# Scores of a head pair as 64-row matmuls on K without zero padding, in a windowed attention kernel with a maxout FFN behind it

## The chip, the core and the metric

The kernel runs on one NeuronCore of a Trainium2 chip. The metric is the time of one execution in device microseconds, as the median over several runs. TensorE appears in the profile as two rows: PE for its matmuls and PEld for the loads of the stationary operand (the weights). The other engines are VectorE (DVE), ScalarE (ACT), GpSimd (POOL) and SyncE (SP), which issues most of the DMAs.

## The reference

Attention over 4 batches, 8 heads, 768 positions and 64 elements per head. A query sees the first 4 positions (the sinks) and the last 128. The heads of a position are then joined to a row of 512 and go through an FFN that takes the elementwise maximum of three products.

```python
scores = scale * np.matmul(q, k.transpose(0, 1, 3, 2))
keep = is_sink | ((rel >= 0) & (rel < 128))      # rel = query position - key position
a = softmax(np.where(keep, scores, -1e9))
x = np.matmul(a, v)          # heads joined: (3072, 512)
h = np.maximum(np.maximum(x @ w1, x @ w2), x @ w3)   # w1, w2, w3: (512, 768)
out = h @ w_out                                      # (768, 512)
```

## The kernel before

The 3072 rows are cut into 12 chunks of 256 positions, three chunks to a batch. Chunk c = 0 of a batch (chunks 0, 3, 6 and 9) has no keys before it. Each chunk goes through the same steps, each a function that emits its instructions when it is called; the order in which the steps are called is written out by hand in strings of short names, and each engine works through its instructions in that order. In "Sb0 Fa1" the first letter is the step, the second says which of the chunks in flight, and the rest is the step's number.

- **K, Q** (`prep`, chunks 0 to 3): K and Q of one half of the heads are transposed on TensorE into PSUM. ACT copies Q to `qT`; `place_k` copies K to `kz` on DVE. For the later chunks **D** (`turn`) transposes by DMA and **E** calls `place_k` on the result.
- **S** (`score`): the scores of one head, with keys on the partitions and queries on the free axis. Q of a pair of heads lies in `qT` with one head on partitions 0 to 63 and the other on 64 to 127. K lies in `kz` twice as wide: for each of the two heads a block of all 128 partitions, where that head's 64 carry K and the other 64 carry zeros. So a matmul with all 128 rows gives the scores of one head. A step has a matmul of 128 columns against the keys of the chunk before (L246, not where c = 0), one of 256 (L248) and one of 128 (L249), into a PSUM tile `st`. ACT takes the exponential of the tile into `e_sb` (L255), and after the second head of a pair DVE multiplies the pair by the mask (L258).
- **Z** (`sink_score`): the scores of the four sinks for all heads (L264) from `ks`, which `sink_k` fills from K at a batch's first chunk.
- **A** (`av`): scores times V into `o_ps` for four heads and 128 positions (L278 for the sinks, L286 for the rest), then a reciprocal and a multiply on DVE (L291, L294) into `x_sb`.
- **T** (`xpose`): `x_sb` transposed on TensorE (L306) and copied by ACT (L307).
- **F** (`ffn_h`): nine steps to a chunk, each eight matmuls of 256 columns (L319). ACT copies the product of w1 to `h_sb` (L323); those of w2 and w3 are joined by DVE with a maximum (L325).
- **Y** (`ffn_y`): the last product (L330), copied by ACT (L335) and stored.

From chunk 2 on one iteration of the loop runs F and Y of a chunk, S, Z, A and T of the next, and the placing of K of the one after. S steps stand singly between F steps:

```python
run("Sb0 Sb1 Fa0 Sb2 Fa1 Sb3 Fa2 Zb Sb4 Fa3 Sb5 Ab00 Fa4 Sb6 Ab01 Fa5 Sb7 Fa6 Fa7 Ab10 "
    "Fa8 Ab11 Ec Ya0 Tb0 Tb1 Ya1", a=i, b=i + 1, c=i + 2)
```

PSUM is given out in three pools that hand their buffers round: `ps_s` with two buffers (scores and sink scores), `ps_o` with two (A, T and the transposes) and `ps_f` with four (F, Y and, in the first two chunks, one score tile of a pair). `e_sb` has six buffers.

Before the loop the strings are longer, the casts of the inputs to bf16 run on POOL and DVE (L181, L189), and the weights arrive. `warm` puts in matmuls whose result nobody reads. The zeros of `kz` are written once: two blocks by DVE (L99), four by ACT (`zeros_act`, L117) and six by POOL (L99).

Of the kernel before, what the change touches and what calls it, by code (L numbers as in the profile page):

```python
# [9 lines left out]
F32 = mybir.dt.float32  # L10
BF16 = mybir.dt.bfloat16
AF = mybir.ActivationFunctionType
ALU = mybir.AluOpType
# [3 lines left out]
def kernel(  # L17
# [13 lines left out]
    nc = tc.nc  # L31
# [8 lines left out]
    scale = 1.0 / (D ** 0.5)  # L40
    NP = H // 2
    CPB = S // 256
# [8 lines left out]
    with tc.manual_schedule():  # L51
        const = tc.alloc_tile_pool(name="const", bufs=1)
        raw = tc.alloc_tile_pool(name="raw", bufs=3)
        work = tc.alloc_tile_pool(name="work", bufs=2)
        ps_s = tc.alloc_tile_pool(name="ps_s", bufs=2, space=bass.MemoryType.PSUM)
        ps_o = tc.alloc_tile_pool(name="ps_o", bufs=2, space=bass.MemoryType.PSUM)
        ps_f = tc.alloc_tile_pool(name="ps_f", bufs=4, space=bass.MemoryType.PSUM)
# [3 lines left out]
        def load(ci, gate=None):  # L61

            b, c = divmod(ci, CPB)
            t0 = c * 256
            eng = nc.sync
            qk = raw.tile([128, 2, 2, 512], F32, tag="qk_raw", name="qk_raw")
            vr = raw.tile([128, 2, H, D], F32, tag="v_raw", name="v_raw")
            if gate is not None:
                gate.memset(qk[0:1, 0, 0, 0:1], 0.0)
            for g in range(2):  # L70
                for j, src in ((0, k), (1, q)):
                    eng.dma_start(  # L72
                        out=qk[:, j, g].rearrange("p (h i d) -> p h (i d)", h=4, d=D),
                        in_=src[b, 4 * g:4 * g + 4, t0:t0 + 256]
                            .rearrange("h (p i) d -> p h (i d)", i=2))
            eng.dma_start(
                out=vr.rearrange("p n h d -> p (n h d)").rearrange("p (h x) -> p h x", h=H),
                in_=v[b, :, t0:t0 + 256].rearrange("h (p i) d -> p h (i d)", i=2))
            raws[ci] = (qk, vr)
# [8 lines left out]
        load(1)  # L88


        kz = [const.tile([128, 2, NP, 256], BF16, name=f"kz{i}") for i in range(2 * CPB)]
        qT = [const.tile([128, 2, NP, 128], BF16, name=f"qT{i}") for i in range(2 * CPB)]
        ve = [const.tile([128, S // 128, H, D + 1], BF16, name=f"ve{i}") for i in range(2)]
        ks = [const.tile([128, NP * 130], BF16, name=f"ks{i}") for i in range(2)]
        vs = const.tile([128, B, H, D + 1], BF16, name="vs")

        def zeros(i, c, eng):
            for h in range(2):
                eng.memset(kz[CPB * i + c][64 - 64 * h:128 - 64 * h, h], 0.0)  # L99

        ident = const.tile([128, 128], BF16, name="ident")
        make_identity(nc, ident)
# [1 line left out]
        def warm(n):  # L104

            wp = ps_f.tile([128, 128], F32, tag="f", name="warm")
            for _ in range(n):
                nc.tensor.matmul(wp, lhsT=ident, rhs=ident, start=True, stop=True)  # L108

        zc = const.tile([128, 1], BF16, name="zc")  # L110
        nc.vector.memset(zc, 0.0)
        zeros(0, 0, nc.vector)

        def zeros_act(i):
            for h in range(2):
                hp = slice(64 - 64 * h, 128 - 64 * h)
                nc.scalar.copy(kz[i][hp, h], zc[hp].unsqueeze(1).to_broadcast([64, NP, 256]))  # L117

        zeros_act(1)
        nc.scalar.copy(vs.rearrange("p b h d -> p (b h d)"), zc.to_broadcast([128, B * H * (D + 1)]))  # L120
        nc.vector.memset(ve[0][:, :, :, D:D + 1], 1.0)
        nc.vector.memset(ks[0], 0.0)
# [2 lines left out]
        msk = const.tile([128, 4, 128], BF16, name="msk")  # L125
        nc.gpsimd.memset(msk[:, 0:2], 1.0)
        for i in range(2):
            for slot, op, sign in ((1, ALU.is_ge, 1), (0, ALU.is_gt, -1)):
                m = msk[64 * i:64 * i + 64, slot].rearrange("p (i t) -> p i t", i=2)
                nc.gpsimd.affine_select(  # L130
                    out=m, in_=m, compare_op=op, fill=0.0, base=-sign * i,
                    pattern=[[sign, 2], [2 * sign, 64]], channel_multiplier=-2 * sign)
        nc.gpsimd.tensor_copy(msk[:, 2:4], msk[:, 0:2])
        msk0 = const.tile([128, 3, 128], BF16, name="msk0")
# [61 lines left out]

        def place_k(ci, src, pairs):

            for h in range(2):
                hp = slice(64 * h, 64 * h + 64)  # L200
                nc.vector.tensor_copy(  # L201
                    kz[ci % (2 * CPB)][hp, h, pairs].rearrange("p a (n i t) -> p i (a n) t", n=2, i=2),
                    src[hp].rearrange("p i a (n t) -> p i (a n) t", n=2))

        def prep(ci, j, g):

# [21 lines left out]
        def sink_k(b):  # L228
            kv = ks[b % 2].rearrange("p (a y) -> p a y", y=130)[:, :, 0:8 * n_sink]
            for h in range(2):  # L230
                for i in range(2):
                    nc.vector.tensor_copy(
                        kv.rearrange("p a (t i x) -> p i a t x", i=2, x=8)[:, i, :, :, h],
                        kz[b * CPB % (2 * CPB)][:, h, :, 64 * i:64 * i + n_sink // 2])

        es = {}

        def score(ci, hd):
            b, c = divmod(ci, CPB)
            p, h = divmod(hd, 2)  # L240
            kh = kz[ci % (2 * CPB)][:, h, p]
            qh = qT[ci % (2 * CPB)][:, :, p].rearrange("p i (n t) -> p n i t", n=2)
            st = (ps_f.tile([128, 4, 128], F32, tag="f", name="st") if ci < 2 and h == 1 else
                  ps_s.tile([128, 4, 128], F32, tag="s", name="st"))
            if c > 0:
                nc.tensor.matmul(st[:, 0], lhsT=kz[(ci - 1) % (2 * CPB)][:, h, p, 128:256],  # L246
                                 rhs=qh[:, 0], start=True, stop=True)
            nc.tensor.matmul(st[:, 1:3], lhsT=kh[:, 0:128], rhs=qh, start=True, stop=True)  # L248
            nc.tensor.matmul(st[:, 3], lhsT=kh[:, 128:256], rhs=qh[:, 1],  # L249
                             start=True, stop=True)  # L250
            if h == 0:
                es[ci, p] = work.tile([128, 2, 4, 128], BF16, tag="e", bufs=6, name="e_sb")
            e = es[ci, p]
            lo = 0 if c > 0 else 1
            nc.scalar.activation(e[:, h, lo:], st[:, lo:], AF.Exp, scale=scale)  # L255
            if h == 1:
                m = (msk if c > 0 else msk0).unsqueeze(1).to_broadcast([128, 2, 4 - lo, 128])
                nc.vector.tensor_tensor(out=e[:, :, lo:], in0=e[:, :, lo:], in1=m, op=ALU.mult)  # L258

        def sink_score(ci):  # L260
            b, c = divmod(ci, CPB)
# [82 lines left out]
        def step(op):  # L344

            name, ci, arg = op[0], int(op[1:3]), op[3:]
            if ci >= NCH:
                return
            if name in "KQ":
                prep(ci, int(name == "Q"), int(arg))  # L350
            elif name == "D":
                turn(ci)
            elif name == "E":
                place_k(ci, kTs.pop(ci), slice(0, NP))
            elif name == "S":
                score(ci, int(arg))
            elif name == "Z":
                if ci % CPB:
                    sink_score(ci)
                elif ci > 0:  # L360
                    sink_k(ci // CPB)
            elif name == "A":
                av(ci, int(arg[0]), int(arg[1]))
            elif name == "T":
                xpose(ci, int(arg))
            elif name == "F":
                ffn_h(ci, int(arg))
            elif name == "Y":
                ffn_y(ci, int(arg))

        def run(text, **at):
            for tok in text.split():
                c = at[tok[1]]
                step(f"{tok[0]}{c:02d}{tok[2:]}")
# [21 lines left out]
        load_w(1)  # L396
        load_w(2)
        load(2, nc.gpsimd)
        run("Sa0 Sa1 Ka1", a=0)
        warm(3)  # L400
        run("Qa1", a=0)
        warm(4)
        run("Sa2 Sa3 Sa4 Sa5", a=0)
        warm(3)
        run("Aa00", a=0)
        warm(2)
        run("Sa6 Sa7 Aa01", a=0)
        warm(2)
        run("Kb0 Qb0 Aa10", a=0, b=1)
        warm(2)  # L410
        run("Aa11", a=0)
        sink_k(0)
        run("Sb0 Sb1 Ta0 Sb2", a=0, b=1)
        warm(6)
        run("Kb1 Qb1", b=1)
        cast_v(1, 1, nc.vector)
        run("Sb3 Ta1 Zb Sb4 Sb5 Sb6 Sb7", a=0, b=1)
        warm(6)
        run("Ab00 Ab01", b=1)
        zeros_act(2)  # L420
        warm(4)
        run("Fa0 Ab10 Fa3 Ab11 Fa6 Tb0 Tb1", a=0, b=1)
        cast_qk(2, 0, 0, nc.gpsimd)
# [4 lines left out]
        cast_v(2, 0, nc.gpsimd)  # L428
        cast_v(2, 1, nc.gpsimd)
        load(3, nc.gpsimd)  # L430
        run("Fa1 Fb0 Fb3 Fb6 Fa4 Fa7 Fb1 Fb4 Fb7 Kc0 Qc0 Fa2 Kc1 Qc1 Fa5 Sc0 Sc1 Fa8 Zc Sc2 Fb2",
            a=0, b=1, c=2)
        for c in range(CPB):
            zeros(1, c, nc.gpsimd)
        nc.gpsimd.memset(ks[1], 0.0)
        nc.gpsimd.memset(ve[1][:, :, :, D:D + 1], 1.0)
        cast(3)
        for b in range(1, B):
            sink_v(b)
        run("Sc3 Sc4 Fb5 Ac00 Sc5 Fb8 Ac01 Sc6 Ya0 Sc7 Ya1", a=0, b=1, c=2)  # L440
        load(4)
        cast(4)
        run("Ac10 Ac11 Yb0 Tc0 Kd0 Tc1 Qd0 Yb1 Kd1 Qd1", b=1, c=2, d=3)
# [1 line left out]
        for i in range(2, NCH):  # L445
            run("Dc", c=i + 2)
            if i + 3 < NCH:
                load(i + 3)
                cast(i + 3)
            run("Sb0 Sb1 Fa0 Sb2 Fa1 Sb3 Fa2 Zb Sb4 Fa3 Sb5 Ab00 Fa4 Sb6 Ab01 Fa5 Sb7 Fa6 Fa7 Ab10 "  # L450
                "Fa8 Ab11 Ec Ya0 Tb0 Tb1 Ya1", a=i, b=i + 1, c=i + 2)

        for pool in (ps_f, ps_o, ps_s, work, raw, const):
            pool.release()
# [35 lines left out]
```

## Time and profile before

| | before |
|---|---|
| median of 4 runs | 197.01 us (196.56 to 197.84) |
| the profiled execution | 197.5 us, of which the span from first to last instruction is 195.8 us |
| granted TensorE clock, mean | 0.985 |
| PE / PEld busy | 183.4 us (94%) / 150.5 us (77%) |
| DVE / ACT / POOL busy | 127.3 us (65%) / 108.6 us (55%) / 79.3 us (41%) |
| DMA moved | 32.85 MB, 168 GB/s in the mean |

Times in the profile's rows are those of single instructions from start to end. On TensorE the ends are modelled, and a matmul's time holds the way through the array, so that matmuls that follow each other overlap in the rows; the distance from one start to the next is what a matmul costs in a full stream. The rows of ACT and DVE overlap a little in the same way. The profiled execution took 197.5 us against the median of 197.01.

### The profile page before, as it was taken

The numbers are of one execution on the slowest core, as the hardware profiler recorded it, in microseconds if no ns is written. First come the engines' busy times: TensorE is split into PE (matmuls) and PEld (weight loads), VectorE is DVE, ScalarE is ACT, GpSimd is POOL, SyncE is SP. The second block draws the span as 40 slices with busy tenths as digits, with TensorE's granted clock in tenths as the row PEclk, the third lists the DMA queues.
The fourth block names the chain that finished last, engine by engine and source line by source line (L and its number), as shares of the span: only waits on it lengthen the run. The fifth ranks groups of instructions, "written<-read, shape, count | busy, mean of one in ns | idle before, by whom it ended". The sixth has DMA issues, their size and how long they took to land.

```text
span 195.8 us, 4740 instructions
## 1 busy us (share of the span) xinstructions
PE 183.4 (94%) x1904; PEld 150.5 (77%) x1916; DVE 127.3 (65%) x275; ACT 108.6 (55%) x202; POOL 79.3 (41%) x133
## 2 busy tenths in 40 slices
PE   7778999999899999999999999999999999999990
PEld 7657788884697798798797897897886996996850
DVE  4699825885379379469479469468476585583520
ACT  8748951453762862862753863863754745744221
POOL 7399105999965543602702625504505500000000
PEclk9978999999999999999999999999999999999997
DMA  5969999893999699298499899497497740400404
GB/s 160 306 186 145 160 216 287 122 279 108 260 280 240 192 200 281 57 170 238 138 111 279 211 153 291 107 224 222 96 224 220 147 71 0 107 3 0 110 2 107
DMA packets 60774, 32.85 MB, mean 168 GB/s; under 512 B 18512, under 2 KB 57680, under 8 KB 60752
## 3 DMA queue, kind: packets, MB, share of 16 engines
q1 hardware_dynamic: 58368, 29.40, 63.2%
q0 software_dynamic: 2384, 3.15, 10.2%
q8 instruction: 15, 0.25, 0.5%
q14 instruction: 7, 0.06, 0.1%
HBM read 25.20 MB, written 6.29 MB: 161 GB/s over the span
## 4 chain that ended last, share of the span: by engine, by line
PE 69%; DMA 9%; POOL 6%; DVE 6%; ACT 2%; issue 2%; SPq 2%; POOLq 0%; DVEq 0%
PE h_ps L319 37%; PE y_ps L330 15%; DMA qk_raw<-in_q_dram 6%; PE o_ps L286 5%; PE st L248 4%; DMA v_raw<-in_v_dram 3%; DVE h_sb L325 3%; DVE e_sb L258 2%; POOL ve L189 2%; PE xt_ps L306 2%; PE st L249 2%; SPq L72 2%; PE sk L264 2%; PE st L246 2%; POOL qk_bf L181 1%
## 5 line engine op out<-in xcount | busy, mean ns | idle before, releaser
L319 PE MATMUL h_ps<-xT,w 128*128 128x256 bf16 x864 | 108.0, 273 | 0.2 <-DMA w<-in_moe_w_dram 0.2
L319 PEld LDWEIGHTS <-w 128*128 128x128 bf16 x864 | 80.2, 98 | 9.3 <-issue 0.4
L255 ACT ACTIVATE e_sb<-st 128x512 bf16<-128x512 f32 (+1 forms) x96 | 52.6, 575 | 19.2 <-PE st L249 18.7
L325 DVE TENSOR_TENSOR h_sb<-h_sb,h_ps 128x512 bf16<-128x512 bf16 x72 | 49.2, 683 | 15.8 <-PE h_ps L319 14.0
L258 DVE TENSOR_TENSOR e_sb<-e_sb,msk 128x1024 bf16<-128x1024 bf16 (+1 forms) x48 | 35.0, 734 | 35.6 <-ACT e_sb L255 35.0
L181 POOL CAST qk_bf<-qk_raw 128x512 bf16<-128x512 f32 x44 | 27.9, 646 | 60.4 <-DMA qk_raw<-in_k_dram 42.8
L189 POOL CAST ve<-v_raw 64x512 bf16<-64x512 f32 x46 | 31.7, 688 | 12.9 <-DMA v_raw<-in_v_dram 9.8
L330 PE MATMUL y_ps<-wo,h_sb 128*128 128x512 bf16 x132 | 34.2, 379 | 0.9 <-DVE h_sb L325 0.3
L335 ACT COPY y_sb<-y_ps 128x512 f32<-128x512 f32 x24 | 14.1, 587 | 37.4 <-PE y_ps L330 31.1
L323 ACT CAST h_sb<-h_ps 128x512 bf16<-128x512 f32 x36 | 21.3, 592 | 12.3 <-PE h_ps L319 12.3
L248 PE MATMUL st<-qT,kz 128*128 128x256 bf16 x96 | 25.3, 275 | 0.8 <-ACT qT L214 0.5
L286 PE MATMUL o_ps<-ve,e_sb 128*128 128x65 bf16 x352 | 20.6, 196 | 2.2 <-DVE e_sb L258 1.1
L330 PEld LDWEIGHTS <-h_sb 128*128 128x128 bf16 x144 | 12.8, 98 | 12.1 <-DVE h_sb L325 1.3
L294 DVE TENSOR_TENSOR x_sb<-o_ps,rc 128x256 bf16<-128x256 f32 x48 | 20.4, 425 | 1.7
L286 PEld LDWEIGHTS <-e_sb 128*128 128x128 bf16 x352 | 17.7, 99 | 4.3 <-DVE e_sb L258 2.0
L249 PE MATMUL st<-qT,kz 128*128 128x128 bf16 x96 | 20.8, 220 | 0.0
L246 PE MATMUL st<-qT,kz 128*128 128x128 bf16 x64 | 14.2, 221 | 0.4 <-ACT e_sink L269 0.3
L307 ACT COPY xT<-xt_ps 128x512 bf16<-128x512 bf16 x24 | 13.3, 601 | 0.5 <-PE xt_ps L306 0.5
L248 PEld LDWEIGHTS <-kz 128*128 128x128 bf16 x96 | 9.4, 98 | 3.5 <-DVE kz L201 0.8
L249 PEld LDWEIGHTS <-kz 128*128 128x128 bf16 x96 | 9.5, 99 | 1.1 <-issue 0.5
L201 DVE COPY kz<-kT 64x1024 bf16<-64x1024 bf16 x16 | 9.6, 599 | 0.3
L108 PE MATMUL warm<-ident 128*128 128x128 bf16 x76 | 8.3, 268 | 1.4 <-POOL ident masks.py:199 1.4
(45 smaller groups left out, 116.0 us busy)
## 6 DMA issues: line engine op xcount, KB each, us to landing
qk_raw<-in_k_dram SPq DMA_DIRECT2D x24, 256.0 KB, 4.2
qk_raw<-in_q_dram SPq DMA_DIRECT2D x24, 256.0 KB, 4.4
v_raw<-in_v_dram SPq DMA_DIRECT2D x12, 512.0 KB, 5.8
out_dram<-y_sb SPq DMA_DIRECT2D x22, 256.0 KB, 3.4
w<-in_moe_w_dram POOLq DMA_DIRECT2D x3, 768.0 KB, 7.7
wo<-in_moe_w_out_dram POOLq DMA_DIRECT2D x2, 384.0 KB, 6.4
out_dram<-y_sb SPq DMA_DIRECT2D x4, 128.0 KB, 2.3
kT<-qk_bf SPq DMA_TRANSPOSE x8, 5.9
```

The source lines that it names most:

```text
L181: eng.tensor_copy(dst.rearrange("p i (h d) -> p h i d", d=D), src)
L189: eng.tensor_copy(dst[64 * i:64 * i + 64], src[64 * n:64 * n + 64, :, i])
L248: nc.tensor.matmul(st[:, 1:3], lhsT=kh[:, 0:128], rhs=qh, start=True, stop=True)
L249: nc.tensor.matmul(st[:, 3], lhsT=kh[:, 128:256], rhs=qh[:, 1], start=True, stop=True)
L255: nc.scalar.activation(e[:, h, lo:], st[:, lo:], AF.Exp, scale=scale)
L258: nc.vector.tensor_tensor(out=e[:, :, lo:], in0=e[:, :, lo:], in1=m, op=ALU.mult)
L286: nc.tensor.matmul(o[:, hh], lhsT=es[ci, p][:, h, sl], rhs=ve[b % 2][:, n, 2 * p + h], start=(c == 0 and x == 0), stop=(x == len(blocks) - 1),
L294: nc.vector.tensor_mul(xs[ci, t][:, 4 * g:4 * g + 4], o[:, :, 0:D], rc.unsqueeze(2).to_broadcast([128, 4, D]))
L319: nc.tensor.matmul(hp[:, f], lhsT=w_sb[wi][:, ds, (2 * fp + f) * 128:(2 * fp + f + 1) * 128], rhs=xTs[ci][:, ds, :], start=(ds == 0), stop ...
L323: nc.scalar.copy(dst, hp)
L325: nc.vector.tensor_max(dst, dst, hp)
L330: nc.tensor.matmul(yp, lhsT=hs[ci][:, fb, t * 128:(t + 1) * 128], rhs=wo[:, fb], start=(fb == 0), stop=(fb == FB - 1))
```

## The change

`kk` takes the place of `kz`: K of a pair of heads, one head on partitions 0 to 63 and the other on 64 to 127, with no zeros, in half the space. `place_k` copies both heads in one instruction, and all writing of zeros goes. `score` handles a pair: its matmuls take 64 partitions of K and of Q, and those of the two heads alternate, each head writing a PSUM tile of its own; both exponentials and the mask follow. In the strings each two S steps become one, so that in the loop four single S steps stand where there were eight. `sink_k` reads the 64 partitions of each head.

```diff
-        kz = [const.tile([128, 2, NP, 256], BF16, name=f"kz{i}") for i in range(2 * CPB)]
+        kk = [const.tile([128, NP, 256], BF16, name=f"kk{i}") for i in range(2 * CPB)]
...
-        zeros(0, 0, nc.vector)
...
-        zeros_act(1)
...
-            for h in range(2):
-                hp = slice(64 * h, 64 * h + 64)
-                nc.vector.tensor_copy(
-                    kz[ci % (2 * CPB)][hp, h, pairs].rearrange("p a (n i t) -> p i (a n) t", n=2, i=2),
-                    src[hp].rearrange("p i a (n t) -> p i (a n) t", n=2))
+            nc.vector.tensor_copy(
+                kk[ci % (2 * CPB)][:, pairs].rearrange("p a (n i t) -> p i (a n) t", n=2, i=2),
+                src.rearrange("p i a (n t) -> p i (a n) t", n=2))
...
-        def score(ci, hd):
+        def score(ci, p):
+
             b, c = divmod(ci, CPB)
...
+            st = [ps_s.tile([128, 4, 128], F32, tag="s", name="st"),
+                  ps_f.tile([128, 4, 128], F32, tag="f", name="st") if ci < 2 else
+                  ps_s.tile([128, 4, 128], F32, tag="s", name="st")]
+            kc, kp = kk[ci % (2 * CPB)], kk[(ci - 1) % (2 * CPB)]
             qh = qT[ci % (2 * CPB)][:, :, p].rearrange("p i (n t) -> p n i t", n=2)
...
+            half = [slice(64 * h, 64 * h + 64) for h in range(2)]
             if c > 0:
...
+                for h, r in enumerate(half):
+                    nc.tensor.matmul(st[h][:, 0], lhsT=kp[r, p, 128:256], rhs=qh[r, 0],
+                                     start=True, stop=True)
+            for h, r in enumerate(half):
+                nc.tensor.matmul(st[h][:, 1:3], lhsT=kc[r, p, 0:128], rhs=qh[r],
+                                 start=True, stop=True)
+            for h, r in enumerate(half):
+                nc.tensor.matmul(st[h][:, 3], lhsT=kc[r, p, 128:256], rhs=qh[r, 1],
+                                 start=True, stop=True)
...
-        run("Sa0 Sa1 Ka1", a=0)
+        run("Sa0 Ka1", a=0)
...
-        run("Sa2 Sa3 Sa4 Sa5", a=0)
+        run("Sa1 Sa2", a=0)
...
-        run("Sa6 Sa7 Aa01", a=0)
+        run("Sa3 Aa01", a=0)
...
-        run("Sb0 Sb1 Ta0 Sb2", a=0, b=1)
+        run("Sb0 Ta0", a=0, b=1)
...
-        run("Sb3 Ta1 Zb Sb4 Sb5 Sb6 Sb7", a=0, b=1)
+        run("Sb1 Ta1 Zb Sb2 Sb3", a=0, b=1)
...
-        zeros_act(2)
...
-        for c in range(CPB):
-            zeros(1, c, nc.gpsimd)
...
-        run("Sc3 Sc4 Fb5 Ac00 Sc5 Fb8 Ac01 Sc6 Ya0 Sc7 Ya1", a=0, b=1, c=2)
+        run("Fb5 Sc2 Ac00 Fb8 Ac01 Ya0 Sc3 Ya1", a=0, b=1, c=2)
...
-            run("Sb0 Sb1 Fa0 Sb2 Fa1 Sb3 Fa2 Zb Sb4 Fa3 Sb5 Ab00 Fa4 Sb6 Ab01 Fa5 Sb7 Fa6 Fa7 Ab10 "
-                "Fa8 Ab11 Ec Ya0 Tb0 Tb1 Ya1", a=i, b=i + 1, c=i + 2)
+            run("Sb0 Fa0 Fa1 Sb1 Fa2 Zb Fa3 Sb2 Ab00 Fa4 Ab01 Sb3 Fa5 Fa6 Fa7 Ab10 Fa8 Ab11 "
+                "Ec Ya0 Tb0 Tb1 Ya1", a=i, b=i + 1, c=i + 2)
```

## The prediction

> **What bounds the kernel now.** I read the page first, then the chain of waits, then busy time by stretches, then the timeline of one iteration.
>
> ```profile
> PE 183.4 (94%) x1904; PEld 150.5 (77%) x1916; DVE 127.3 (65%) x275; ACT 108.6 (55%) x202; POOL 79.3 (41%) x133
> PE 69%; DMA 9%; POOL 6%; DVE 6%; ACT 2%; issue 2%; SPq 2%; POOLq 0%; DVEq 0%
> ```
>
> TensorE carries 69% of the chain that ended last. In order of time that chain runs over DMAs and POOL casts until 35.99 us, and from there almost wholly over matmuls. The busy times by stretches (length, then PE, PEld, DVE, ACT, POOL) say the same:
>
> ```profile
> 10.00:20.00 10.00, 8.10 (x97) 6.52 (x95) 9.63 (x22) 6.40 (x15) 9.78 (x14) 0.83 0.80 165
> 36.00:50.00 14.00, 12.98 (x133) 9.91 (x134) 10.18 (x21) 7.34 (x14) 13.32 (x20) 1.00 0.82 189
> 81.20:95.60 14.40, 14.35 (x156) 11.95 (x154) 9.76 (x20) 8.34 (x17) 4.43 (x8) 1.00 0.92 183
> 108.90:123.40 14.50, 14.45 (x157) 12.07 (x156) 10.05 (x20) 8.44 (x17) 5.98 (x9) 1.00 0.88 196
> ```
>
> In an iteration of 14.5 us PE lacks 0.05; DVE and ACT have 4 to 6 us left. So after 36 us the kernel is worth what its matmul stream is worth. The start of an iteration in the timeline (start, duration):
>
> ```profile
> 108.34 0.22 PE L246 MATMUL st<-qT,kz 128*128 128x128 bf16 x1
> 108.40 0.27 PE L248 MATMUL st<-qT,kz 128*128 128x256 bf16 x1
> 108.51 0.22 PE L249 MATMUL st<-qT,kz 128*128 128x128 bf16 x1
> 108.56 0.22 PE L246 MATMUL st<-qT,kz 128*128 128x128 bf16 x1
> 108.62 0.27 PE L248 MATMUL st<-qT,kz 128*128 128x256 bf16 x1
> 108.73 0.22 PE L249 MATMUL st<-qT,kz 128*128 128x128 bf16 x1
> 108.78 1.04 PE L319 MATMUL h_ps<-xT,w 128*128 128x256 bf16 x8
> ```
>
> A head's three matmuls take 0.22 us from start to start (108.34 to 108.56), and F follows with no hole. A matmul of 128 columns costs 0.055 in the stream but lasts 0.22: some 0.166 us is the way through the array (0.27 minus 0.11 for 256 columns gives the same). These 0.166 us are hidden as long as the next matmul may enter behind the last.
>
> **Scores in half the stream.** From chunk 2 on there are ten chunks: seven with c > 0 (0.22 us a head) and three with c = 0, where the second head starts 0.17 after the first (52.58 and 52.75). If the two heads of a pair run side by side, a pair costs one head's time: 7 x 4 x 0.22 = 6.2, and 3 x 4 x 0.17 = 2.0, together 8.2 us saved. All matmuls of the trace have 128 rows, so no row shows two side by side; the bounds are 8.2 and nothing. I take 8.2, since the two use different rows and write different PSUM tiles. The Trainium skill, TensorE: Matmul & The Clock Gate, Part 3, reports matmuls on distinct row groups starting about 4 ns apart; no row here shows it, and by it the saving would be the same 8.2 less 0.5 for 120 second matmuls.
>
> **Changing between 128 and 64 rows.** Every S step now stands between steps of 128 rows, so ten chunks have 40 S steps and 80 changes. What a change costs no row shows. Low end, nothing: between matmuls and transposes the stream goes on without a hole (chain of waits: start, length):
>
> ```profile
> 105.74 1.03 PE y_ps L330 x4
> 106.76 0.45 PE xt_ps L306 x8
> 107.21 1.29 PE y_ps L330 x6
> ```
>
> A gain from the change itself I exclude: it adds no work that could run earlier. High end: the array must be empty (0.166) and the weights are loaded only then. What an unhidden load costs shows where A waited for the mask:
>
> ```profile
> 103.78 0.45 PEld L286 LDWEIGHTS <-e_sb 128*128 128x128 bf16 x4
> 103.89 0.47 PE L286 MATMUL o_ps<-ve,e_sb 128*128 128x65 bf16 x4
> ```
>
> 0.11 us from load to matmul, so 0.276 in all. I take 0.166, between the ends: I expect the halves' results to leave the array by another way than the full column's, which asks for an empty array but not for late weights. 80 x 0.166 = 13.3 us. The Trainium skill, TensorEngine Tiling (Array Packing), Key Properties, speaks against this change: changing the tiling mode drains TensorE. It gives no figure and no run here has shown it; by it the sum is 13.3 us or more on this side, and without it the sum would be the 8.2 saved alone.
>
> **Waits that the pairs add.** A pair needs both buffers of `ps_s`, so its second head waits for the second exponential of the pair before, and behind it on PE all F, A and Z steps queue. I walk an iteration without holes from 108.34 = 0. The exponentials start when ACT is through the Y copy, at 0.68 (109.02), and go at 0.5 each (two took 1.10): buffers free at 1.28 and 1.78. Fa0 and Fa1 (0.87 each) end at 1.97: no wait. S1 exponentials end at 3.0 and 3.5; Fa2 ends at 3.07, so Z finds its buffer. S2 runs at 4.38, ACT first copies Fa3, the exponentials end at 5.66 and 6.16; PE comes to S3 at 6.18: 0.05 of wait. DVE then has mask 2 (0.63 in the stream), two reciprocals and multiplies (0.54 a pair), a maximum (0.59) and mask 3, done at 9.2; PE reaches Ab10 at 9.06 and waits 0.24. Some 0.3 us an iteration, 0.2 where c = 0: 2.7 in ten. With 0.33 us of holes at each S step PE comes later than all of these, and they vanish. Vanishing too are waits that PE has today: the windows from 36 to 180 us lack 2.1 us of PE in all, of which I count half, 1.0, as regained.
>
> **DVE, ACT, POOL.** `place_k` goes from two copies to one of the same length per partition: 8 x 0.599 (from DMA) and 8 x 0.420 (from PSUM) = 8.2 us of DVE time, hidden: in an iteration it runs at 106.46 for a chunk that S reads one iteration later. If that cover were gone, it would be a gain of 0.6 an iteration. The zeros: POOL 6 x 0.948 at 38.19 to 44.08, after which the chain has no POOL step; ACT 4 x 1.044, two of them at 21.51, where PE soon waits for weights (a DMA, 26.17); DVE 2 x 0.485 before the first data. Nothing of it on the path. `sink_k` keeps 16 copies of 0.230.
>
> **The start.** Before 36 us there are six groups of S steps, 12 changes, 12 x 0.166 = 2.0 us, against 4 x 0.17 + 4 x 0.22 = 1.6 saved. PE has 1.9 us of idle time at 10 to 20 us alone, and the release at 36 us is POOL's and a DMA's. I put it at nothing; without that cover it is +0.4.
>
> **The sum.** -8.2 + 13.3 - 1.0 = +4.1 us on the profiled 197.5 (195.8 of span and 1.7 around it): 201.6. The median of the runs is 0.5 lower, so 201.1; I say 201.0.
>
> **Rivals.**
> - *The change of rows is cheap* (under 0.08 us). For it: changes to and from transposes cost nothing. Against it: a matmul is 0.166 us under way, and something must keep results of two row counts apart. At nothing: -8.2 + 2.7 = -5.5, 191.5; at 0.05 the four microseconds of holes fall partly into the waits of the walk, some -4, 193. It decides below about 0.11 us a change, where 80 changes equal 8.2 plus 1.0 less a rest of waits of some 0.4.
> - *Weights load only after emptying* (0.276). 80 x 0.276 = 22.1, -8.2, -1.5 of waits: +12.4, 209.4. For it: PEld is today a step ahead of PE and each S step would lose that twice. Against it: loads into other rows need not disturb.
> - *The halves do not run side by side*, only alternate. The stream is as long as today; with emptied array 13.3 - 2 = +11.3, 208.3, with free changes near 197. For it: no row of two matmuls at once. Against it: different rows, different PSUM tiles.
>
> **How the numbers follow.** The forecast (a change costs 0.13 to 0.22 us; own range 198.5 to 206) gets 0.37; the cheap change 0.33; late weights 0.14; no side by side 0.09, mostly slower; a change near the balance of 0.11 us 0.07. A measurement of this kernel tells 0.5% (1 us) from no change: faster 0.33, same 0.07, slower 0.60. The range runs from 191.0, the cheap case with fewer waits than in the walk, to 209.0; a tenth lies above and less below.
>
> **What would show it.** In the changed profile the score rows must read 64 rows, the two heads of a pair must start within a few ns, and a pair must last 0.22 us from its first start to the end of its stream. From an S step's last matmul to the next start there should be about 0.22 us (0.055 of stream and 0.166 of hole) where today there is 0.055, and the same hole ahead of the step. PE waits for `e_sb` and ACT should shrink. The prediction is wrong if F starts 0.06 us after S (then ACT and DVE waits should appear at Ab10), if the holes are near 0.28 with the loads inside them, or if the second head starts a full stream after the first.

## The result, and the profile after

| | before | after |
|---|---|---|
| median | 197.27 us (63 runs) | 196.56 us (44 runs) |
| ratio to before | | 0.9966 (95%: 0.9953 to 0.9979) |
| profiled execution | 197.5 us, span 195.8 | 197.5 us, span 195.8 |

The change brings a third of a percent, 0.7 us. The forecast was 201.0; the time lies in the stated range, but the change is a small gain and not a loss of 4 us, near the point where saving and cost balance. The profiled execution of the changed kernel is 1 us above its median, so the two pages show the same span; the reading below goes by the inside of the loop, which repeats exactly.

The page of the changed kernel, busy time of the engines and share of the chain that ended last:

```profile
PE 182.9 (93%) x1904; PEld 137.9 (70%) x1916; DVE 117.3 (60%) x257; ACT 103.3 (53%) x198; POOL 73.6 (38%) x127
PE 77%; DMA 8%; DVE 4%; POOL 4%; issue 2%; ACT 2%; SPq 1%
```

DVE, ACT and POOL lost 10, 5 and 6 us of work, and TensorE's share of the chain grew. The windows of the changed kernel (length, then PE, PEld, DVE, ACT, POOL, and at the end granted clock, DMA share and GB/s):

```profile
10.00:20.00 10.00, 8.31 (x86) 5.93 (x86) 9.02 (x21) 5.78 (x14) 9.64 (x15) 0.66 0.84 173
36.00:50.00 14.00, 12.96 (x138) 8.70 (x137) 9.34 (x19) 6.57 (x13) 8.90 (x16) 1.00 0.81 185
81.20:95.60 14.40, 14.35 (x156) 10.91 (x156) 9.38 (x19) 8.27 (x17) 4.86 (x8) 1.00 0.92 183
108.90:123.40 14.50, 14.45 (x157) 10.90 (x156) 8.89 (x19) 8.37 (x17) 6.20 (x11) 1.00 0.89 196
```

PE is as busy as before, 14.45 of 14.50, but these rows cannot show what happened: a matmul's row holds its 0.166 us of way through the array, so a hole in the stream that is shorter than that is covered by the row of the matmul ahead of it. PEld does not show it either: 12.07 us of loads in this stretch became 10.90, but the loads of the scores alone went from 2.34 to 1.17, since those of the two halves now lie over each other, and that is the whole difference. The timeline shows the hole itself, the time between the end of one stream and the start of the next matmul (start, duration; x2 are the two heads):

```profile
113.06 1.04 PE L310 MATMUL h_ps<-xT,w 128*128 128x256 bf16 x8
114.03 0.23 PE L236 MATMUL st<-qT,kk 64*128 64x128 bf16 x2
114.10 0.27 PE L239 MATMUL st<-qT,kk 64*128 64x256 bf16 x2
114.20 0.22 PE L242 MATMUL st<-qT,kk 64*128 64x128 bf16 x2
114.36 0.28 PE L269 MATMUL o_ps<-vs,e_sink 128*128 128x260 bf16 x1
```

Eight matmuls of F take 8 x 0.109 us of stream and end at 113.93; the first score starts at 114.03, 0.10 later. The two heads start together (4 ns apart in the single starts). The last score's stream ends at 114.26 and the next step starts at 114.36. In the single starts, over the 32 S steps from 66 to 180 us, the hole ahead is 0.096 us and the one behind 0.093, whether a matmul of 65, 256 or 512 columns stands ahead and whoever follows (their streams, from start to start elsewhere in this trace, are 0.029, 0.109 and 0.216 us). Besides, the first matmul after each change holds the stream a little longer than the same matmul elsewhere: by 0.012 us after going in, and by 0.010 after coming out, where 256 columns take 0.119 instead of 0.109. The loads, from the same timeline's PEld rows:

```profile
114.03 0.10 PEld L236 LDWEIGHTS <-kk 64*128 64x128 bf16 x2 [0.21 <-issue]
114.35 0.10 PEld L269 LDWEIGHTS <-e_sink 128*128 128x128 bf16 x1 [0.16 <-issue]
```

The load of the other row count waits as well, and then starts with its matmul (4 ns ahead in the single starts): it is not drawn ahead, and no load lies in the hole. Changes between matmuls and transposes still cost nothing (chain of waits, changed kernel):

```profile
121.01 1.03 PE y_ps L321 x4
122.03 0.45 PE xt_ps L297 x8
122.48 1.29 PE y_ps L321 x6
```

A pair thus takes 0.424 us from the end of the stream ahead to the next step's start, against 0.442 before, and the 0.010 of the matmul behind come on top. Where c = 0 it is 0.367 against 0.330. The saving is there and the changes eat it.

### The profile page after: what moved, and what is told of

It reads as the page before. It is cut to its first block, busy times and chain, and to the rows that moved or that the text cites. A ratio compares the mean times of both kernels' runs of the same rounds, so it can differ in the third digit from the quotient of the medians.

```text
span 195.8 us, 4711 instructions
## 1 busy us (share of the span) xinstructions
PE 182.9 (93%) x1904; PEld 137.9 (70%) x1916; DVE 117.3 (60%) x257; ACT 103.3 (53%) x198; POOL 73.6 (38%) x127
## 4 chain that ended last, share of the span: by engine, by line
PE 77%; DMA 8%; DVE 4%; POOL 4%; issue 2%; ACT 2%; SPq 1%
PE h_ps L310 45%; PE y_ps L321 15%; DMA w<-in_moe_w_dram 4%; PE o_ps L277 4%; DMA v_raw<-in_v_dram 3%; PE st L239 3%; PE xt_ps L297 2%; PE st L236 2%; PE o_ps L269 2%; POOL ve L177 2%; DVE h_sb L316 2%; PE sk L255 2%; PE st L242 1%; DVE e_sb L249 1%; ACT e_sb L247 1%
## 5 line engine op out<-in xcount | busy, mean ns | idle before, releaser
L310 PE MATMUL h_ps<-xT,w 128*128 128x256 bf16 x864 | 104.5, 273 | 0.3 <-DMA w<-in_moe_w_dram 0.3
L247 ACT ACTIVATE e_sb<-st 128x512 bf16<-128x512 f32 (+1 forms) x96 | 48.8, 567 | 14.7 <-PE st L242 14.7
L177 POOL CAST ve<-v_raw 64x512 bf16<-64x512 f32 x46 | 30.7, 668 | 14.6 <-DMA v_raw<-in_v_dram 12.7
L277 PE MATMUL o_ps<-ve,e_sb 128*128 128x65 bf16 x352 | 19.5, 195 | 2.4 <-DVE e_sb L249 1.3
L239 PE MATMUL st<-qT,kk 64*128 64x256 bf16 x96 | 13.6, 279 | 0.8 <-ACT qT L200 0.5
L242 PE MATMUL st<-qT,kk 64*128 64x128 bf16 x96 | 10.8, 220 | 0.0
L200 ACT COPY qT<-pt 128x512 bf16<-128x512 bf16 x8 | 4.7, 588 | 9.9 <-PE pt L198 9.9
L269 PE MATMUL o_ps<-vs,e_sink 128*128 128x260 bf16 x32 | 8.8, 277 | 0.6 <-DVE x_sb L285 0.6
L282 DVE RECIPROCAL rc<-o_ps 128x4 f32<-128x4 f32 x48 | 8.5, 176 | 1.6 <-PE o_ps L277 1.5
L297 PEld LDWEIGHTS <-x_sb 128*128 128x128 bf16 x96 | 6.6, 100 | 3.6 <-issue 1.2
```

The costliest lines, as they stand in the source:

```text
L177: eng.tensor_copy(dst[64 * i:64 * i + 64], src[64 * n:64 * n + 64, :, i])
L239: nc.tensor.matmul(st[h][:, 1:3], lhsT=kc[r, p, 0:128], rhs=qh[r], start=True, stop=True)
L247: nc.scalar.activation(e[:, h, lo:], st[h][:, lo:], AF.Exp, scale=scale)
L277: nc.tensor.matmul(o[:, hh], lhsT=es[ci, p][:, h, sl], rhs=ve[b % 2][:, n, 2 * p + h], start=(c == 0 and x == 0), stop=(x == len(blocks) - 1),
L310: nc.tensor.matmul(hp[:, f], lhsT=w_sb[wi][:, ds, (2 * fp + f) * 128:(2 * fp + f + 1) * 128], rhs=xTs[ci][:, ds, :], start=(ds == 0), stop ...
```

## The experiments

Theory A: a change of rows costs about 0.097 us wherever it stands, 80 of them eat the 8.2 us that two streams side by side save. Against it stood that the holes are waits for buffers (B), that a change costs the 0.166 of the prediction (C), and that side by side saves nothing.

### Changes added elsewhere

In `ffn_h`, ahead of the eight matmuls of four F steps; the second run has 128 rows in place of 64:

```diff
+            if ci >= 2 and n in (1, 3, 6, 8):
+                nc.tensor.matmul(hp[:, 0, 0:64], lhsT=ident[0:64], rhs=ident[0:64, 0:64],
+                                 start=True, stop=True)
```

> The changed kernel with 40 small matmuls more (64 rows, 64 columns, ahead of the eight of F1, F3, F6 and F8 in chunks 2 to 11, all between steps of 128 rows; what they write is overwritten). Theory A (a change between 128 and 64 rows costs about 0.097 us whatever stands on either side): each adds two changes and 0.027 us of stream, 40 x 0.22 = 8.8 us: about 205.4 us, and in the trace a hole of 0.098 us ahead of each and 0.095 behind. Theory B (the holes at the S steps are waits for score buffers or exponentials): nothing to wait for here, as e2, about 197.8. Theory C (a change costs the 0.166 of the prediction, partly hidden at the S steps): 40 x 0.36 = 14.4 us, 211.

> The same 40 small matmuls with 128 rows: no change of rows. All theories: 40 x 0.03 = 1.2 us, about 197.8 us. e1 less e2 is then the price of 80 changes: theory A 7.7 us, B 0, C 13.3.

Measured 205.53 us with 64 rows, ratio 1.0425 (1.0390 to 1.0461), and 197.49 with 128, 1.0035 (1.0014 to 1.0056), beside 196.65 of the kernel before. The difference is 8.0 us for 80 changes, 0.10 each (7.7 us by the ratios). The timeline with 64 rows:

```profile
98.03 1.05 PE L313 MATMUL h_ps<-xT,w 128*128 128x256 bf16 x8
99.01 0.20 PE L309 MATMUL h_ps<-ident 64*128 64x64 bf16 x1
99.14 1.05 PE L313 MATMUL h_ps<-xT,w 128*128 128x256 bf16 x8
```

and with 128:

```profile
94.66 1.05 PE L313 MATMUL h_ps<-xT,w 128*128 128x256 bf16 x8
95.54 0.19 PE L309 MATMUL h_ps<-ident 128*128 128x64 bf16 x1
95.57 0.82 PE L313 MATMUL h_ps<-xT,w 128*128 128x256 bf16 x6
```

With 128 rows the small matmul costs 0.03 us; with 64 rows 0.13 lie between its start and the next, and 0.10 ahead of it. The same matmul in the same buffer has no hole with 128 rows, so B falls, and C's 211 us is out of reach. A stands.

### One half after the other

```diff
-            if c > 0:
-                for h, r in enumerate(half):
+            for h, r in enumerate(half):
+                if c > 0:
                     nc.tensor.matmul(st[h][:, 0], lhsT=kp[r, p, 128:256], rhs=qh[r, 0],
                                      start=True, stop=True)
-            for h, r in enumerate(half):
                 nc.tensor.matmul(st[h][:, 1:3], lhsT=kc[r, p, 0:128], rhs=qh[r],
                                  start=True, stop=True)
-            for h, r in enumerate(half):
                 nc.tensor.matmul(st[h][:, 3], lhsT=kc[r, p, 128:256], rhs=qh[r, 1],
                                  start=True, stop=True)
```

> The changed kernel, but in a pair all three matmuls of the first head come ahead of those of the second, so that only the last of one and the first of the other can run side by side. Theory A (side by side is what saves): a pair's stream becomes 0.38 instead of 0.22 us (c > 0) and 0.27 instead of 0.17: 28 x 0.16 + 12 x 0.11 = 5.8 us more, about 202.4. Rival (starts 4 ns apart are only records; the streams follow each other anyway): no difference, 196.6.

Measured 196.57 us, ratio 0.9982 (0.9960 to 1.0004): 5.8 us less than theory A expected, and the rival's number. But the trace shows that neither was tested. The timeline of this run:

```profile
112.31 0.24 PE L236 MATMUL st<-qT,kk 64*128 64x128 bf16 x2
112.38 0.28 PE L238 MATMUL st<-qT,kk 64*128 64x256 bf16 x2
112.49 0.23 PE L240 MATMUL st<-qT,kk 64*128 64x128 bf16 x2
112.64 0.28 PE L267 MATMUL o_ps<-vs,e_sink 128*128 128x260 bf16 x1
```

The program has the second head's three matmuls behind all three of the first. Nevertheless both L236 start 10 ns apart, ahead of either L238, and so on for each counterpart. So the second head's first matmul started ahead of two that stand before it in the program: across the two halves TensorE did not keep to that order here. A pair lasts 0.430 us. The order within a pair does not matter, and whether side by side saves had to be asked in another way.

### Both heads on one half

```diff
-            half = [slice(64 * h, 64 * h + 64) for h in range(2)]
+            half = [slice(0, 64) for h in range(2)]
```

> The changed kernel, but the second head of a pair takes the first head's K and Q, on the lower 64 partitions (the odd heads' scores are left out); all matmuls of a pair then need the same half of TensorE's rows. Theory A (what saves is that two halves stream side by side): 28 x 0.22 + 12 x 0.17 = 8.2 us more, 204.8 us. Rival (64-row matmuls of whatever half overlap, or the stream is not what counts): 196.6.

Measured 205.90 us, ratio 1.0457 (1.0397 to 1.0517). The timeline of this run:

```profile
117.11 0.28 PE L236 MATMUL st<-qT,kk 64*128 64x128 bf16 x2
117.24 0.38 PE L239 MATMUL st<-qT,kk 64*128 64x256 bf16 x2
117.45 0.27 PE L242 MATMUL st<-qT,kk 64*128 64x128 bf16 x2
117.66 0.29 PE L269 MATMUL o_ps<-vs,e_sink 128*128 128x260 bf16 x1
```

Two on one half follow each other: 0.13, 0.21 and 0.21 us in place of 0.07, 0.10 and 0.16. In the loop a chunk takes 15.35 us instead of 14.48 (13.86 instead of 13.21 where c = 0), so ten chunks make 7 x 0.87 + 3 x 0.65 = 8.0 us, against 8.2 expected. The rest of the 9 us goes with the clock of single runs: two of the four took 204.40 (the profiled one) and 204.76 us at a granted clock of 0.99 and 0.98, the other two 207.05 and 207.34 at 0.96. The profiled one lies 7.8 us above the changed kernel's median. The saving of the prediction is real and was sized right.

### The order of the steps, and the zeros

The first of these two runs has the new strings and the alternating order in `score`, but `kz`, its zeros and matmuls of 128 rows; the second is the changed kernel with all zeros written to a tile that nobody reads, and with K placed by two copies.

> The new order of the steps, with K padded, the zeros, and matmuls of 128 rows as before: no change of rows, nothing side by side. Theory A (80 changes x 0.097 = 7.8 us eat 8.2 saved): nearly the time of the changed kernel, 196.6 to 197.3. If the halves had no cost of changing, this kernel would be 8.2 us above the changed one; if there were no saving, 7.8 below. Within the 0.7 us: 196.6 if the order brings it, 197.3 if the rows or the zeros do.

> The changed kernel with all work on zeros put back (into a tile that nobody reads, at the old places on DVE, ACT and POOL) and with K placed in two copies of 64 partitions as before. If that work is off the path, as the prediction had it: 196.6 us. If it is what the small gain of 0.7 us comes from: 197.3.

Measured 197.03 us, ratio 1.0005 (0.9988 to 1.0023), and 197.72, ratio 1.0042 (1.0015 to 1.0069). The new order alone leaves the time as it was. A pair of 128-row matmuls in the timeline of the first:

```profile
113.54 0.28 PE L250 MATMUL st<-qT,kz 128*128 128x128 bf16 x2
113.65 0.38 PE L253 MATMUL st<-qT,kz 128*128 128x256 bf16 x2
113.87 0.28 PE L256 MATMUL st<-qT,kz 128*128 128x128 bf16 x2
113.98 0.27 PE L283 MATMUL o_ps<-vs,e_sink 128*128 128x260 bf16 x1
```

0.44 us without a hole, nearly as long as the changed kernel's 0.42 with two. The second run says that the work taken away was not all hidden: with it the changed kernel is no faster than the kernel before. So it was put back in parts, beside the changed kernel itself (the comments say which run has the line; the definitions are left out):

```diff
+        zeros(0, 0, nc.vector)      # DVE, and ACT's four: first run
+        zeros_act(1)
...
+        zeros_act(2)
...
+        for c in range(CPB):        # POOL's six: second run
+            zeros(1, c, nc.gpsimd)
...
+            for h in range(2):      # two copies of 64 partitions: third run
+                hp = slice(64 * h, 64 * h + 64)
+                nc.vector.tensor_copy(kk[ci % (2 * CPB)][hp, pairs]...
```

> The changed kernel with only the zeros of DVE and ACT back (two blocks and four, before 24 us). If these are what made the run with all of that work back 1.5 us slower than the changed kernel: about 1 us above the changed kernel of this set. If they are hidden, as the prediction had it: equal to it.

> The changed kernel with only the six zero blocks of POOL back (5.9 us of POOL ahead of the casts of chunk 3). Hidden: equal to the changed kernel. On the path (K and V of chunk 3 come late): about 1 us above.

> The changed kernel with K placed by two copies of 64 partitions instead of one of 128. Hidden: equal to the changed kernel. On the path in the first chunks, where the matmuls wait for K from PSUM: 0.3 to 1 us above.

> The changed kernel itself, beside the three parts. From its first measurement 0.34% under the kernel before. Should it come out nearer to the kernel before, or the three parts lie on both sides of it by as much, then the 1.5 us of the run with all of that work back is the scatter of sets and not that work.

| put back | median | ratio to before |
|---|---|---|
| zeros of DVE and ACT | 196.73 us | 0.9985 (0.9964 to 1.0006) |
| zeros of POOL | 196.58 us | 0.9978 (0.9959 to 0.9997) |
| two copies of K | 197.46 us | 1.0024 (1.0007 to 1.0041) |
| nothing: the changed kernel | 196.54 us | 0.9959 (0.9932 to 0.9986) |

The zeros are hidden as far as these runs can tell: 0.2 us and nothing by the medians, 0.5 and 0.4 by the ratios, with intervals that overlap the changed kernel's. The second copy of K costs 0.9 us (1.3 by the ratios), with intervals that do not touch, and that is as much as the whole gain. It is not the clock: the medians of the granted clock in the 12 runs of each are 0.988 with two copies and 0.986 without. The loop of the run with two copies (length, PE, PEld, DVE, ACT, POOL, clock, DMA share, GB/s), and of the changed kernel measured again:

```profile
66.00:180.00 114.00, 113.58 (x1197) 84.90 (x1204) 75.85 (x166) 64.88 (x128) 35.99 (x54) 1.00 0.70 157
66.00:180.00 114.00, 113.58 (x1198) 85.44 (x1205) 72.26 (x159) 64.54 (x128) 35.68 (x53) 1.00 0.71 154
```

In the loop both run alike (113.58 of 114 us, and 14.48 us a chunk in each). So the 0.9 us arise outside it, and 0.3 of them at the very end. The last maxima on DVE (start, duration), with two copies and then in the changed kernel measured again:

```profile
187.51 0.69 DVE L318 TENSOR_TENSOR h_sb<-h_sb,h_ps 128x512 bf16<-128x512 bf16 x1 [1.13 <-PE h_ps L312]
188.66 0.69 DVE L318 TENSOR_TENSOR h_sb<-h_sb,h_ps 128x512 bf16<-128x512 bf16 x1 [0.45 <-PE h_ps L312]
186.00 1.49 DVE L316 TENSOR_TENSOR h_sb<-h_sb,h_ps 128x512 bf16<-128x512 bf16 x2 [1.13 <-PE h_ps L310]
```

With two copies the last maximum starts 0.34 us later, and the last Y waits for it. No wait in the profile shows the reason, and K was placed long before. The kernel before, the run with all that work back and the padded run have 0.35 us of such idle time at the same place, the changed kernel and the two runs with zeros have none. But the padded run with two pairs together, which has two copies, has none either, and the run with 40 matmuls of 64 rows more, which has one, has some. So whether the second copy brings it is not shown. The other 0.6 us lie ahead of 66 us, where DVE copies K out of PSUM before the first scores; at which step is not settled. The scores' waits for K on PE are no longer with two copies (0.9 us in all ahead of 66 us, against 1.1).

### Two pairs together

```diff
+            if ci > 2 and p % 2 == 1:
+                st = [ps_f.tile([128, 4, 128], F32, tag="f", name="st") for _ in range(2)]
...
+            run("Sb0 Sb1 Fa0 Fa1 Fa2 Zb Fa3 Ab00 Sb2 Sb3 Fa4 Ab01 Fa5 Fa6 Ab10 Fa7 Fa8 Ab11 "
+                "Tb0 Ya0 Ec Tb1 Ya1", a=i, b=i + 1, c=i + 2)
```

> The changed kernel with two S steps next to each other in the loop (S0 S1 and S2 S3, the odd ones in buffers of ps_f), so chunks 3 to 11 have two changes to 64 rows and back instead of four, and F, A, Y, T moved a little. Theory A: 9 x 4 x 0.097 = 3.5 us less, 193.1 us if nothing else waits. Theory B (buffers and exponentials make the holes): two pairs in a row wait more, 196.6 or above.

> The order of the run with two S steps together, with K padded and matmuls of 128 rows. Theory A: a pair costs 0.445 us of TensorE here and 0.323 there (a group of two lasts 0.646 with its two holes), 9 chunks x 4 x 0.12 = 4.4 us more than that run's 192.7: 197.1. If that run's gain came from the order of the steps and not from fewer changes: 193.

Measured 192.72 us, ratio 0.9791 (0.9755 to 0.9828), and for the same order with padded K 196.27, ratio 0.9968 (0.9948 to 0.9988). A group of two pairs in the timeline of the first:

```profile
147.96 0.23 PE L239 MATMUL st<-qT,kk 64*128 64x128 bf16 x2
148.03 0.27 PE L242 MATMUL st<-qT,kk 64*128 64x256 bf16 x2
148.14 0.22 PE L245 MATMUL st<-qT,kk 64*128 64x128 bf16 x2
148.19 0.22 PE L239 MATMUL st<-qT,kk 64*128 64x128 bf16 x2
148.25 0.27 PE L242 MATMUL st<-qT,kk 64*128 64x256 bf16 x2
148.36 0.22 PE L245 MATMUL st<-qT,kk 64*128 64x128 bf16 x2
148.51 0.72 PE L313 MATMUL h_ps<-xT,w 128*128 128x256 bf16 x5
```

The second pair follows the first with no hole (148.14 to 148.19), and two pairs cost 0.643 us with the holes at both ends, where two padded ones cost 0.883. With 44 changes instead of 80 the time is, by the ratios, 3.4 us less than the changed kernel's: theory A again (3.5), and the fastest version of this study, ahead of both kernels. Against the kernel before it is 4.1 us less; the order alone brings 0.6 us of that, and the rest, 3.5 us, needs the 64 rows. The expectation for the padded run was 4.4 us above the other: it took the price of a c > 0 pair for all chunks.

## Why the prediction was wrong

- **The saving, 8.2 us: right.** The two halves stream side by side; taking that away cost 8.0 us in the ten chunks.
- **The change of rows, 80 x 0.166 = 13.3 us: the step that failed.** It is 0.096 us going in and 0.093 coming out: 40 x 0.189 = 7.6 us, 5.7 less. That a change leaves a hole in the stream is the mechanism named. Its size was taken from the wrong row: a matmul's 0.166 us from the end of its stream to its own end is longer than what the next one has to wait. The Trainium skill, TensorEngine Tiling (Array Packing), Key Properties, states that a change of the tiling mode drains TensorE. A change costs 0.10 us here, but that the array is empty by then the rows do not show: the first score starts at 114.03, 0.07 us ahead of the modelled end of the matmul before it (113.06 + 1.04). Nor does any run show that the halves' results leave the array by another way, which was the reason for choosing 0.166. The high end, 0.276 with a load behind the emptying, fell too: load and matmul start together. The case that came true, a change near the balance of 0.11 us, had been given 0.07.
- **The first matmul after each change, not in the sum.** The 0.012 us inside a pair and the 0.010 behind it make 40 x 0.022 = 0.9 us.
- **Waits regained, 1.0 us, and the start, put at nothing.** The run with the new order and padded K shows both without a change of rows. From Z of chunk 4 to Z of chunk 11 its profile takes 98.66 us, that of the kernel before 99.36: 0.7 of waits regained. But Z of chunk 4 comes at 70.16 instead of 69.50, and the whole time is the same (1.0005). So the start gives back what the loop gains. Where in the start, one profile of each does not settle.
- **Zeros hidden: right. `place_k` hidden: wrong.** The cover was argued for the copies in the loop, whose result is read an iteration later, and carried over to the eight copies out of PSUM ahead of it. One copy instead of two makes -0.9 us, in the profiles 0.6 of it ahead of 66 us and 0.3 at the end; by which way stays open.

With the measured terms, and the new order at nothing: -8.2 + 7.6 + 0.9 - 0.9 = -0.6 us, against -0.7 (-0.9 to -0.4 by the interval). That this comes out so near is in part luck: the second copy's 0.9 and the new order's nothing are each uncertain by some 0.3 us. A count in the prediction was off too, without weight: ten chunks have 108 second matmuls and not 120, and the 4 ns between the heads count once in a pair.

## What to carry to other kernels

Two 64-row matmuls on the halves of TensorE's rows do halve their stream, but a group of them pays a fixed 0.19 us for going in and out, and 0.02 more at the first matmul after each change: it must save more than that, so put as many together as PSUM has tiles for, and count the groups, not the matmuls. A single pair of heads with 512 columns each saves 0.22 and is even; with two pairs together the kernel gained 2%. A busy share of TensorE near 100% does not exclude such holes: compare the start of a matmul with the start and columns of the one ahead. And whether work that is hidden in the loop is hidden in the start too has to be asked again.

## What the runs showed of the hardware

- A change between 128 and 64 rows leaves a hole of 0.096 us going in, the same after matmuls of 65, 256 and 512 columns, and of 0.093 us coming out (0.105 after the single matmul of 64 columns). The first matmul after it takes 0.010 to 0.012 us more. A change to transposes costs nothing.
- Matmuls on the other half of the rows passed those ahead of them in program order: with three behind three, each started 10 ns after its counterpart. The Trainium skill, TensorE: Matmul & The Clock Gate, Part 3, says that matmuls start and end in program order; across the halves this run does not agree, and the measurement decides.
- Kernels whose scores have 64 rows were granted a lower clock: the median over a set's runs is 0.972 to 0.988 in the eleven sets with them, 0.995 to 0.997 in the three sets of the kernel before whose runs list a clock and in the two padded runs. Of the changed kernel's 44 runs the 22 with the lower clock have a median of 196.81 us, the others 196.33. What lowers the clock, and whether it costs the changed kernel part of its gain, no run settles.
